# A mixture-of-experts kernel whose last stretch is ranked by explicit waits: left sums, right products between stored groups, last rows in stores of 3, 6 and 9

## The chip, the cores and the metric

The kernel runs on one core of one Trainium2 chip. The metric is the device time of one execution, in microseconds (us). The kernel before takes 205.71 us, the median of three runs (205.70 to 205.94).

A core has five instruction streams that run side by side and meet through semaphores: TensorE (PE, matrix products; its weight loads are shown as PEld), VectorE (DVE), ScalarE (ACT), GpSimd (POOL) and SyncE (SP), which here issues all the transfers. Transfers run on 16 DMA engines. Products land in the eight banks of PSUM; VectorE and ScalarE copy them to SBUF, and from SBUF they are stored to HBM.

## The reference

An attention with pooled keys and values feeds a soft mixture of experts:

```python
logits = x @ phi                                  # x: 4608 x 512, phi: 512 x 32
d = softmax(logits, axis=0)                       # over the 4608 rows
slot_input = d.T @ x                              # 32 slots, 4 for each of 8 experts
for e in range(8):
    h = np.maximum(slot_input[e] @ w1[e], 0.0)    # 4 x 1024, w1[e]: 512 x 1024
    slot_out[e] = h @ w2[e]                       # w2[e]: 1024 x 512
c = softmax(logits, axis=1)                       # over the 32 slots
return c @ slot_out                               # 4608 x 512, float32
```

Everything is float32. The weights w1 and w2 are 33.6 MB, the output is 9.4 MB. The change touches only the end: the second products of the experts, the transposes of `c`, and the last product with its stores.

## The kernel before

The program isn't written in the order in which it runs. Every piece of work is handed to a planner (`Plan.add`) with its engine, an assumed cost, what it reads and writes, and a rank. `Plan.order` then goes through an assumed time line and takes, each time, the piece that can start first; of those that can start at once, the one with the lowest rank. The order that comes out is the order of the instructions on each engine. An engine executes its instructions in that order and waits where an operand is not there yet.

The attention runs over four pairs of batches and is the first two thirds of the time. It leaves the logits, one tile for each pair (`L[0]` to `L[3]`), and the slot inputs `SIM`. What follows is the part that matters here.

- **First products.** `expert_in` multiplies the slots with `w1`, two loads of 1 MB for each expert; `hidden` applies the maximum and turns the result into `hTb`.
- **Second products.** `w2` comes as 16 pieces of 1 MB, two for each expert. A piece serves the left half of the 512 output columns (d = 0, sum in the bank `kvbank`) and the right half (d = 1, sum in `scbank`). `mult` (line 1396) makes eight matrix instructions for one piece and one half. The first 12 pieces are loaded whole (8 KB in a row for each partition). The last four (`NT = 4`, the tails) are loaded in halves by `tail_out`: for each half of the columns and each tail two loads of 256 KB with 1 KB in a row, all the left ones ahead of all the right ones.
- **Keep-warm products.** `keep_warm` (line 1382) adds a product whose result nobody reads, with the lowest rank, for the pieces 6 to 11 and for seven of the eight tail products: 13 in all.
- **Slot weights.** `slots(bp)` computes the softmax over the 32 slots for a pair (VectorE, ScalarE), splits it into a rounded part and a rest, and transposes both on TensorE (line 1508, five matrix instructions for a pair) into `cT[bp]`. Two buffers hold the splits, so that of pair 3 waits for the transposes of pair 1. For the first pair it also keeps an exact transposed copy `c4` of the first three rows j (`ND = 3`). The transposes of pairs 1 to 3 have a rank (`TURN = 30000`) behind that of all other work of the end.
- **Slot sums.** `slot_sums` copies a bank to SBUF (line 1311), adds its four row groups with one product (line 1320), and ScalarE and VectorE split the sum into a rounded part and a rest, `sr` (lines 1577 and 1582).
- **Output.** A partition holds nine output rows, j = 0 to 8, for each pair of batches, 36 in all. `direct` (line 1555) makes the left half of rows 0 to 2 of pair 0 from `c4` and the bank's copy, without waiting for the slot sums, and stores each by itself (line 1567, 128 KB). The other rows come from `out_mult` (line 1591): two matrix instructions for each row. `evict` copies a product to SBUF, rows with odd j on ScalarE (line 1546) and rows with even j on VectorE (line 1547). Three rows form a group. The first six groups (`NA = 6`) are made and stored in halves, left halves first (384 KB a store with 1 KB in a row, line 1603); the other six groups are made at full width and stored as 768 KB with 6 KB in a row.

All loads and stores go through SP's one queue. Which right products stand between which output rows is left to the planner's time line; all have lower ranks than the output rows and are taken as soon as it thinks that their load has landed.

The lines of the code that the change and the prediction touch: `NT, NA` 1290, `slot_sums` 1306, `keep_warm` 1379, `mult` 1389, `expert_out` 1405, `tail_out` 1424, `slots` 1452, `direct` 1550, `out_mult` 1588, `store` 1600, the loops over groups 1610 to 1641.

Of the kernel before, what the change touches and what calls it, by code (L numbers as in the profile page):

```python
# [20 lines left out]
class Plan:  # L21
# [23 lines left out]

    def add(self, eng, cost, fn, r=(), w=(), also=(), pri=None, dma=0.0, slack=0.0):
        cost, ni = cost if isinstance(cost, tuple) else (cost, 4)
# [29 lines left out]
        self.ops.append((eng, cost, fn, deps, pri, dma, tiles, need, slack, ni))  # L77

    def order(self):
# [189 lines left out]
def kernel(  # L269
# [24 lines left out]
    nc = tc.nc  # L294
# [950 lines left out]
    def over(shape, n):  # L1245
# [43 lines left out]
    EG = 4  # L1289
    NT, NA = 4, 6  # L1290
    hTb = hTs.tile().split(E // EG)
# [13 lines left out]

    def slot_sums():
        for d in range(2):
            x = slice(d * HD, d * HD + HD)
            add(
                *((ACT, act(HD)) if d else (DVE, dve(HD))),  # L1310
                lambda d=d, x=x: (nc.scalar.copy if d else nc.vector.tensor_copy)(
                    accs.ap[:, x], pacc[d].ap[:, 0, :HD]
                ),
                r=[pacc[d]], w=[accs.part(d)],
            )
            if d == 0:
                direct(0, 1)
            add(
                PE, 0.5,
                lambda d=d, x=x: nc.tensor.matmul(  # L1320
                    so[d].ap[:, :HD], rep.rearrange("p a n -> p (a n)"), accs.ap[:, x],
                    start=True, stop=True,
                ),
                r=[accs.part(d), rep_b], w=[so[d]],
            )

# [97 lines left out]
    def tail_out():  # L1424
        for d in range(2):
            for e, i, t in tails:
                w2h = w2[e].rearrange("(i p j t) d -> p i j t d", i=2, j=2, t=2)
                for j in range(2):
                    load(
                        lambda j=j, d=d, t=t: t.ap.rearrange("p (j t d) -> p j t d", j=2, t=2)[  # L1430
                            :, j, :, d * HD: d * HD + HD
                        ],
                        w2h[:, i, j, :, d * HD: d * HD + HD], 1 << 18, t.part(2 * d + j),
                    )
        for d in range(2):
            for e, i, t in tails:
                add(
                    PE, (0.45, 16),
                    lambda d=d, e=e, i=i, t=t: mult(pacc[d].ap[:, 0], e, i, t, d),
                    r=[hTb.part(e // EG), t.part(2 * d), t.part(2 * d + 1)], w=[pacc[d]],  # L1440
                )
                if (d, e, i) != (1, E - 1, 1):
                    keep_warm([t.part(2 * d), t.part(2 * d + 1)])

# [3 lines left out]
    cT = {}  # L1448
    TURN = 30000
    c4 = c4s.tile()  # L1450

    def slots(bp):
# [82 lines left out]
    for e in range(E):  # L1535
        expert_out(e)
        if e < NBP:
            slots(e)
    tail_out()


# [7 lines left out]

    def direct(i0, i1):  # L1550
        for i in range(i0, i1):
            po, ot = b_o.tile(), half[0]
            add(
                PE, 0.45,
                lambda po=po, i=i: nc.tensor.matmul(
                    po.ap[:, :HD], c4.ap[:, i * P: i * P + P], accs.ap[:, :HD],
                    start=True, stop=True,
                ),
                r=[accs.part(0), c4], w=[po], also=[ot],
            )  # L1560
            add(
                *evict(lambda i=i: ot.ap[:, i * DM: i * DM + HD], po, HD, i % 2),
                r=[po], w=[ot.part(i)],
            )
            add(
                SP, 0.06,
                lambda i=i: nc.sync.dma_start(outv[:P, i, :HD], ot.ap[:, i * DM: i * DM + HD]),
                r=[ot.part(i)], dma=P * HD * 4 / HALF_RATE,
            )

    outv = out.rearrange("(p j) d -> p j d", j=J)
    slot_sums()
    direct(1, ND)
    for d in range(2):
        x = slice(d * HD, d * HD + HD)
        add(
            ACT, act(HD), lambda x=x, d=d: nc.scalar.copy(sr.ap[:, 0, x], so[d].ap[:, :HD]),
            r=[so[d]], w=[sr.part(d)],
        )
        add(  # L1580
            DVE, dve(HD),
            lambda x=x, d=d: nc.vector.tensor_tensor(
                sr.ap[:, 1, x], so[d].ap[:, :HD], sr.ap[:, 0, x].bitcast(F32), op=ALU.subtract
            ),
            r=[so[d], sr.part(d)], w=[sr.part(d)],
        )

    def out_mult(bp, j, po, x):
# [10 lines left out]

    def store(bp, j0, x, ot, r):  # L1600
        add(
            SP, 0.06,
            lambda: nc.sync.dma_start(
                outv[bp * P: bp * P + P, j0: j0 + G, x],
                ot.ap.rearrange("p (g d) -> p g d", g=G)[:, :, x],
            ),
            r=r, dma=P * G * (x.stop - x.start) * 4 / (DMA_RATE if x.stop - x.start == DM else HALF_RATE),
        )

    for d in range(2):  # L1610
        x = slice(d * HD, d * HD + HD)
        for (bp, j0), ot in zip(groups, half):
            if (bp, j0, d) == (0, 0, 0):
                continue
            for i in range(G):
                po = b_o.tile()
                add(
                    PE, 0.22,
                    lambda po=po, bp=bp, j=j0 + i, x=x: out_mult(bp, j, po, x),
                    r=[sr.part(d), cT[bp]], w=[po], also=[ot],  # L1620
                )
                y = i * DM + d * HD
                add(
                    *evict(lambda ot=ot, y=y: ot.ap[:, y: y + HD], po, HD, (j0 + i) % 2),
                    r=[po], w=[ot.part(G * d + i)],
                )
            store(bp, j0, x, ot, [ot.part(G * d + i) for i in range(G)])
    for bp, j0 in groups[NA:]:
        ot = ots.tile().split(G)
        for i in range(G):  # L1630
            po = b_o.tile()
# [8 lines left out]
            )  # L1640
        store(bp, j0, slice(0, DM), ot, [ot])

# [30 lines left out]
```

## Time and profile before

| what | value |
|---|---|
| median of three runs | 205.71 us |
| the profiled execution's own time | 205.98 us |
| its span, first to last instruction | 204.1 us |
| its instructions | 6131 |
| TensorE busy | 176.8 us (87% of the span) |
| VectorE busy | 134.6 us (66%) |
| ScalarE busy | 70.3 us (34%) |
| DMA, mean over the span | 375 GB/s |
| read from HBM / written | 66.65 MB / 9.44 MB |

The profile is one execution. Times in it are counted from the start of its span. The view by stretches gives, for each stretch of time, the busy time of each engine with the number of its instructions, the granted clock of TensorE (1.00 is full speed), the mean busy share of the 16 DMA engines, and what they moved in GB/s. The chain of waits is followed back from the last instruction: at each step to whatever released it. A line number stands for the line of the program that made the instruction.

### The profile page before, as it was taken

How to read it: one execution, taken by the hardware profiler on the slowest of the kernel's cores; microseconds unless marked ns; L12 is line 12 of the kernel's file. 1: busy time of each engine (PE TensorE's matmuls, PEld its weight loads, DVE VectorE, ACT ScalarE, POOL GpSimd, SP SyncE). 2: the span in 40 equal slices, each digit the busy share in tenths (PEclk: the TensorE clock that was granted, in tenths of full speed). 3: DMA queues.
4: the chain of work that ended last, by engine and by line, in shares of the span. 5: the costliest groups of instructions: out<-in, count | busy, mean ns of one | idle time of the engine just before them, and what ended most of it. 6: DMA issues, size and time to landing. Idle time of an engine off the chain costs nothing.

```text
span 204.1 us, 6131 instructions
## 1 busy us (share of the span) xinstructions
PE 176.8 (87%) x2645; PEld 114.5 (56%) x2645; DVE 134.6 (66%) x243; ACT 70.3 (34%) x188; POOL 84.3 (41%) x84
## 2 busy tenths in 40 slices
PE   7999638988699899798999788989999999999960
PEld 6677535646456486455575456455566635576640
DVE  7822540799897899999899985579942004578600
ACT  2022404446441855517373250201202005466400
POOL 7199205589992994799844482000000000000000
PEclk9999996999969999999999999999999999999995
DMA  6999999999999999999999999999999999599993
GB/s 203 368 391 392 382 387 384 386 387 382 395 382 390 384 391 388 384 396 398 406 392 413 409 409 409 414 430 413 425 413 422 372 311 333 198 338 340 412 410 151
DMA packets 33579, 76.49 MB, mean 375 GB/s; under 512 B 2064, under 2 KB 14864, under 8 KB 32016
## 3 DMA queue, kind: packets, MB, share of 16 engines
q1 hardware_dynamic: 33552, 76.09, 99.1%
q8 instruction: 21, 0.34, 0.7%
q14 instruction: 6, 0.05, 0.1%
HBM read 66.65 MB, written 9.44 MB: 373 GB/s over the span
## 4 chain that ended last, share of the span: by engine, by line
PE 38%; DMA 22%; DVE 14%; POOL 11%; issue 4%; SPq 4%; ACT 2%; POOLq 1%; DVEq 0%
DMA arena<-in_moe_w_dram 14%; DMA arena<-in_v_dram 9%; PE bank L1591 6%; PE scbank L811 6%; PE kvbank L702 4%; PE bank L880 4%; SPq L500 4%; POOL arena L846 3%; POOL arena L667 3%; PE scbank L1382 3%; POOL arena L646 3%; POOL arena L869 3%; PE bank L1008 2%; DVE arena L604 2%; DVE arena L825 2%
## 5 line engine op out<-in xcount | busy, mean ns | idle before, releaser
L646 POOL TENSOR_TENSOR arena<-arena 128x1152 f32<-128x1152 f32 x8 | 21.0, 2636 | 17.7 <-ACT arena L639 15.2
L589 DVE STREAM_TRANSPOSE arena<-top 128x1152 f32<-128x1152 f32 x16 | 21.6, 1354 | 8.2 <-DMA top<-in_q_dram 8.2
L702 PE MATMUL kvbank<-arena 64*32 64x128 f32 x1152 | 21.0, 278 | 6.5 <-issue 2.3
L811 PE MATMUL scbank<-arena 64*64 64x288 f32 x256 | 23.7, 447 | 2.3 <-DVE arena L825 2.3
L518 PE MATMUL kvbank<-ones 128*128 128x256 f32 x82 | 23.6, 424 | 2.4 <-ACT arena L726 1.3
L667 POOL TENSOR_TENSOR arena<-arena 128x128 f32<-128x128 f32 (+2 forms) x32 | 23.4, 732 | 3.2 <-ACT arena L655 1.3
L702 PEld LDWEIGHTS kvbank<-arena 64*32 64x32 f32 x1152 | 16.5, 107 | 11.1 <-issue 5.3
L869 POOL TENSOR_TENSOR arena<-arena,ssm 128x576 f32<-128x576 f32 x16 | 18.3, 1153 | 9.5 <-DVE ssm L865 7.9
L846 POOL TENSOR_TENSOR arena<-arena,smx 128x576 f32<-128x576 f32 x16 | 18.4, 1155 | 7.7 <-DVE smx L841 7.7
L604 DVE TENSOR_REDUCE arena<-arena 128x128 f32<-128x1152 f32 x8 | 17.1, 2151 | 4.4 <-DMA arena<-in_phi_dram 4.2
L880 PE MATMUL bank<-arena 128*128 128x288 f32 x64 | 18.8, 425 | 1.2 <-DVE arena L872 0.8
L518 PEld LDWEIGHTS kvbank<-ones 128*128 128x128 f32 x82 | 15.8, 208 | 6.1 <-ACT arena L726 1.7
L1547 DVE COPY arena<-bank 128x256 f32<-128x256 f32 (+1 forms) x30 | 14.2, 509 | 5.5 <-PE bank L1591 3.7
L825 DVE STREAM_TRANSPOSE arena<-scbank 128x576 f32<-128x576 f32 x16 | 12.2, 764 | 5.6 <-PE scbank L811 5.6
L811 PEld LDWEIGHTS scbank<-arena 64*64 64x64 f32 x256 | 9.9, 141 | 10.2 <-DVE arena L825 3.7
L1591 PE MATMUL bank<-sr,cT 64*128 64x256 f32 (+1 forms) x102 | 14.6, 355 | 0.5 <-DVE arena L1547 0.3
L851 ACT ACTIVATE arena<-arena 128x576 f32<-128x576 f32 x16 | 10.9, 684 | 11.2 <-POOL arena L846 11.1
L880 PEld LDWEIGHTS bank<-arena 128*128 128x128 f32 x64 | 11.2, 189 | 6.4 <-DVE arena L872 1.8
L1336 PE MATMUL bank<-arena,SIM 128*32 128x256 f32 x224 | 13.2, 390 | 0.4 <-DVE SIM L1231 0.4
L1591 PEld LDWEIGHTS bank<-sr,cT 64*128 64x128 f32 x102 | 10.1, 185 | 5.6 <-DVE arena L1547 4.4
L872 DVE STREAM_TRANSPOSE arena<-arena 128x576 f32<-128x576 f32 x16 | 11.9, 752 | 1.3 <-POOL arena L869 1.3
L856 DVE TENSOR_REDUCE ssm<-arena 128x18 f32<-128x576 f32 x16 | 11.8, 739 | 1.1 <-ACT arena L851 0.8
(139 smaller groups left out, 255.9 us busy)
## 6 DMA issues: line engine op xcount, KB each, us to landing
arena<-in_moe_w_dram SPq DMA_DIRECT2D x26, 1024.0 KB, 14.8
top<-in_q_dram SPq DMA_DIRECT2D x8, 1152.0 KB, 12.3
arena<-in_k_dram SPq DMA_DIRECT2D x8, 1152.0 KB, 10.1
arena<-in_v_dram SPq DMA_DIRECT2D x8, 1152.0 KB, 12.6
arena<-in_phi_dram SPq DMA_DIRECT2D x8, 576.0 KB, 7.1
out_dram<-arena SPq DMA_DIRECT2D x6, 768.0 KB, 8.9
out_dram<-arena SPq DMA_DIRECT2D x11, 384.0 KB, 3.2
arena<-in_moe_w_dram SPq DMA_DIRECT2D x16, 256.0 KB, 5.7
```

Of the source, the lines that this page charges most:

```text
L518: lambda: nc.tensor.matmul(warm.ap, ones, ones.unsqueeze(1).to_broadcast([P, 2, P]), start=True, stop=True,),
L589: lambda: nc.vector.transpose(qT.ap.rearrange("p (i u y) -> p u i y", i=2, y=Y), qt.ap[:, h * QT_SZ: h * QT_SZ + QT_SZ].rearrange("p (u i ...
L604: lambda: nc.vector.tensor_reduce(mx.ap[:, c0:c1], ph().rearrange("p c j m -> p c m j"), axis=AX.X, op=ALU.max),
L646: lambda: nc.gpsimd.tensor_tensor(ph(), ph(), mb.ap[:, c0:c1].unsqueeze(2).to_broadcast([P, c1 - c0, J, M]), op=ALU.subtract,),
L667: plus = lambda o, x, y: nc.gpsimd.tensor_tensor(o, x, y, op=ALU.add)
L702: nc.tensor.matmul(acc.ap[M * c: M * c + M, a, : 2 * D], ph()[h0: h0 + HALF, c, j, :], kv()[h0: h0 + HALF, :, c, j * D: j * D + D], start= ...
L811: nc.tensor.matmul(scb.ap[HALF * g: HALF * g + HALF, a, :JY], pair[g].kd.ap[h0: h0 + HALF, i, c].rearrange("p r m -> p (r m)"), pair[g].qT ...
L825: lambda: nc.vector.transpose(ex.ap[:, c * PART: (c + 1) * PART].rearrange("p (a x) -> p a x", a=2), scb.ap[:, :, :JY],),
L846: lambda: nc.gpsimd.tensor_tensor(exv(), exv(), bc(mx), op=ALU.subtract),
L869: lambda: nc.gpsimd.tensor_tensor(exv(), exv(), bc(sm), op=ALU.mult),
L880: nc.tensor.matmul(lp.ap[:, :JY], vpb.ap[:, h, :], aT.ap[:, a * JY: (a + 1) * JY], start=(h == 0), stop=(h == H - 1),)
L1591: nc.tensor.matmul(po.ap[:, : x.stop - x.start], cT[bp].ap[y: y + HALF, j // 2 * P: j // 2 * P + P], sr.ap[y: y + HALF, t, x], start=(t == 0),
```

## The change

- `Plan.add` takes a list `after` of further pieces of work to wait for, and returns the number of the piece.
- Five tails instead of four: piece 11 too is loaded in halves.
- The transposes of pairs 1 and 2 come after the left product of the first tail, those of pair 3 after that of the second (`TURN`); their rank is now an ordinary one.
- `slot_sums(d)` does one half whole, splitting included. The left half comes first, ahead of `direct`.
- `direct` makes two rows instead of three. The third row of the first group is made by `out_mult`, and stored by itself.
- The right product of the first tail comes after the second `direct` row; those of the second and third after the left half of group 1; those of the fourth and fifth after that of group 2 (`RIGHT`). Then the right half's slot sums.
- The tail products have no keep-warm products any more; six are left, for the pieces 5 to 10.
- The 18 rows of pairs 2 and 3 are stored by 3, 6 and 9 rows (6, 12 and 18 KB in a row for each partition) instead of six times 3. The two large ones get areas of their own in SBUF.

```diff
-    def add(self, eng, cost, fn, r=(), w=(), also=(), pri=None, dma=0.0, slack=0.0):
+    def add(self, eng, cost, fn, r=(), w=(), also=(), pri=None, dma=0.0, slack=0.0, after=()):
...
+        deps.update(after)
...
+    b0 = W0 + NOUT * OT_SZ
+    big = {6: area(b0, [6 * DM], 1, [ws]), 9: area(b0 + 6 * DM, [9 * DM], 1, [ws])}
...
-    ND = 3
+    ND = 2
...
-    NT, NA = 4, 6
+    NT, NA = 5, 6
+    TURN = {1: 0, 2: 0, 3: 1}
+    RIGHT = (-1, 1, 1, 2, 2)
+    SLOT_AT = (20.06, 20.08, 20.1)
...
+    def slot_sums(d, middle=lambda: None):
+        x = slice(d * HD, d * HD + HD)
...
+        add(
+            ACT, act(HD), lambda: nc.scalar.copy(sr.ap[:, 0, x], so[d].ap[:, :HD]),
+            r=[so[d]], w=[sr.part(d)],
+        )
...
-                if (d, e, i) != (1, E - 1, 1):
-                    keep_warm([t.part(2 * d), t.part(2 * d + 1)])
+
+    def tail_mult(d, n, after=()):
+        e, i, t = tails[n]
+        return add(
+            PE, (0.45, 16), lambda: mult(pacc[d].ap[:, 0], e, i, t, d),
+            r=[hTb.part(e // EG), t.part(2 * d), t.part(2 * d + 1)], w=[pacc[d]], after=after,
+        )
...
-                pri=TURN + 10 * bp + t if bp >= 1 else None,
+                after=turn_at[bp],
...
-        if e < NBP:
-            slots(e)
+        if e == 0:
+            slots(0)
     tail_out()
+    for n in range(NT):
+        x = tail_mult(0, n)
+        for bp in range(1, NBP):
+            if TURN[bp] == n:
+                turn_at[bp].append(x)
+    for bp in range(1, NBP):
+        plan.at(SLOT_AT[bp - 1])
+        slots(bp)
+    plan.at(21)
...
+    z = slot_sums(0)
+    for i in range(ND):
+        z = direct(i, [z])
+    for n in range(-1, NA):
+        if n >= 0:
+            z = half_group(0, n, n == 0)
+        for m in range(NT):
+            if RIGHT[m] == n:
+                tail_mult(1, m, [z])
+        if RIGHT[NT - 1] == n:
+            slot_sums(1)
+    for n in range(NA):
+        half_group(1, n)
+    for bp, j0, n in ((2, 0, 3), (2, 3, 6), (3, 0, 9)):
+        ot = (ots if n == G else big[n]).tile().split(n)
+        for i in range(n):
...
-        store(bp, j0, slice(0, DM), ot, [ot])
+        store(bp, j0, slice(0, DM), ot, [ot], None, n)
```

`half_group(d, n, single)` makes the rows of one group's half as the loop before did; with `single` it starts at row `ND` and stores each row by itself.

More of the change, by code (lines that the diff above doesn't have):

```diff
@@ L1304 @@
     so = [b_l.tile(), Tile(ap=kvbank[:, 1])]
[L1306 to L1325, printed above, removed]
+    def slot_sums(d, middle=lambda: None):
+        x = slice(d * HD, d * HD + HD)
+        add(
+            *((ACT, act(HD)) if d else (DVE, dve(HD))),
+            lambda: (nc.scalar.copy if d else nc.vector.tensor_copy)(
+                accs.ap[:, x], pacc[d].ap[:, 0, :HD]
+            ),
+            r=[pacc[d]], w=[accs.part(d)],
+        )
+        y = middle()
+        z = add(
+            PE, 0.5,
+            lambda: nc.tensor.matmul(
+                so[d].ap[:, :HD], rep.rearrange("p a n -> p (a n)"), accs.ap[:, x],
+                start=True, stop=True,
+            ),
+            r=[accs.part(d), rep_b], w=[so[d]], after=[y] if y is not None else (),
+        )
+        add(
+            ACT, act(HD), lambda: nc.scalar.copy(sr.ap[:, 0, x], so[d].ap[:, :HD]),
+            r=[so[d]], w=[sr.part(d)],
+        )
+        add(
+            DVE, dve(HD),
+            lambda: nc.vector.tensor_tensor(
+                sr.ap[:, 1, x], so[d].ap[:, :HD], sr.ap[:, 0, x].bitcast(F32), op=ALU.subtract
+            ),
+            r=[so[d], sr.part(d)], w=[sr.part(d)],
+        )
+        return z
     def expert_in(e, hb):
@@ L1434, in tail_out @@
                     )
[L1435 to L1441, printed above, removed]
-                if (d, e, i) != (1, E - 1, 1):
-                    keep_warm([t.part(2 * d), t.part(2 * d + 1)])
+    def tail_mult(d, n, after=()):
[3 more added lines that the diff above has]
+            r=[hTb.part(e // EG), t.part(2 * d), t.part(2 * d + 1)], w=[pacc[d]], after=after,
+        )
     cmxs = sb("cmx", [P, J], 1)
@@ L1448 @@
     cT = {}
-    TURN = 30000
+    turn_at = {bp: [] for bp in range(NBP)}
     c4 = c4s.tile()
@@ L1548, in evict, with direct @@
         )
[L1550 to L1578, printed above, removed]
-        )
-        add(
[L1581 to L1585, printed above, removed]
-        )
+    def direct(i, after=()):
+        po, ot = b_o.tile(), half[0]
+        x = add(
+            PE, 0.45,
+            lambda: nc.tensor.matmul(
+                po.ap[:, :HD], c4.ap[:, i * P: i * P + P], accs.ap[:, :HD],
+                start=True, stop=True,
+            ),
+            r=[accs.part(0), c4], w=[po], also=[ot], after=after,
+        )
+        add(
+            *evict(lambda: ot.ap[:, i * DM: i * DM + HD], po, HD, i % 2 == 0),
+            r=[po], w=[ot.part(i)],
+        )
+        store(0, i, slice(0, HD), ot, [ot.part(i)], i)
+        return x
     def out_mult(bp, j, po, x):
@@ L1598, in out_mult, with store @@
             )
-    def store(bp, j0, x, ot, r):
+    def store(bp, j0, x, ot, r, i=None, g=G):
+        n, k = (g, 0) if i is None else (1, i)
         add(
@@ L1608, in store @@
         )
[L1610 to L1626, printed above, removed]
-            store(bp, j0, x, ot, [ot.part(G * d + i) for i in range(G)])
@@ L1628, with half_group @@
-    for bp, j0 in groups[NA:]:
-        ot = ots.tile().split(G)
-        for i in range(G):
+    def half_group(d, n, single=False):
+        (bp, j0), ot, x = groups[n], half[n], slice(d * HD, d * HD + HD)
+        for i in range(ND if single else 0, G):
+            po = b_o.tile()
+            z = add(
+                PE, 0.22, lambda po=po, j=j0 + i: out_mult(bp, j, po, x),
+                r=[sr.part(d), cT[bp]], w=[po], also=[ot],
+            )
+            y = i * DM + d * HD
+            add(
+                *evict(lambda y=y: ot.ap[:, y: y + HD], po, HD, (j0 + i) % 2),
+                r=[po], w=[ot.part(G * d + i)],
+            )
+            if single:
+                store(bp, j0 + i, x, ot, [ot.part(G * d + i)], i)
+        if not single:
+            store(bp, j0, x, ot, [ot.part(G * d + i) for i in range(G)])
+        return z
@@ new lines @@
+    outv = out.rearrange("(p j) d -> p j d", j=J)
+    z = slot_sums(0)
[14 more added lines that the diff above has]
+        for i in range(n):
```

7 lines of the change are left out of this document (4 added, 3 removed).

## The prediction

> **What bounds the kernel now.** I read the page first, then its last third by stretches, the chain of waits there, and SP's transfers.
>
> ```profile
> span 204.1 us, 6131 instructions
> PE 176.8 (87%) x2645; PEld 114.5 (56%) x2645; DVE 134.6 (66%) x243; ACT 70.3 (34%) x188; POOL 84.3 (41%) x84
> q8 instruction: 21, 0.34, 0.7%
> ```
> ```profile
> 150.00:157.00 7.00, 7.00 (x127) 4.70 (x123) 1.58 (x4) 1.63 (x5) 0.00 (x0) 1.00 1.02 425
> 167.00:172.00 5.00, 4.99 (x47) 2.43 (x41) 1.72 (x4) 2.40 (x9) 0.00 (x0) 1.00 1.06 346
> 172.00:173.00 1.00, 1.00 (x8) 0.68 (x4) 0.04 (x1) 0.19 (x1) 0.00 (x0) 1.00 0.93 313
> 173.00:175.00 2.00, 2.00 (x18) 0.99 (x17) 0.94 (x3) 0.69 (x3) 0.00 (x0) 1.00 0.55 184
> 175.00:177.00 2.00, 2.00 (x25) 1.07 (x24) 1.23 (x4) 0.89 (x3) 0.00 (x0) 1.00 0.36 117
> 177.00:189.00 12.00, 11.48 (x85) 8.21 (x82) 9.41 (x22) 7.57 (x19) 0.00 (x0) 1.00 1.02 340
> 190.00:200.00 10.00, 6.99 (x32) 5.27 (x30) 1.98 (x3) 1.33 (x3) 0.00 (x0) 0.99 1.02 412
> 200.00:201.00 1.00, 0.00 (x0) 0.00 (x0) 0.00 (x0) 0.00 (x0) 0.00 (x0) 0.50 0.80 326
> 201.00:202.00 1.00, 0.00 (x0) 0.00 (x0) 0.00 (x0) 0.00 (x0) 0.00 (x0) 0.50 0.06 25
> ```
>
> The last two columns tell the story. Whole pieces come at 425 GB/s, halves with 1 KB in a row at 346, and stores leave at 340 (1 KB) and 412 (6 KB). The transfers are the bound everywhere but from 173 to 177, where they move 368 + 234 = 602 KB in 4 us: at 340 GB/s that is 1.8 us of work, so 2.2 us are lost. There the loads are through and the stores not yet made. From 176.7 an unbroken stream of stores sets the end: eleven half groups of 393 KB (1.157 us each at 340) and 18 full rows of 262 KB (11.45 us at 412) end at 176.7 + 12.7 + 11.45 = 200.9, where the rate drops. (Begin of the stream: from 175 to 177 go 234 KB, of which 131 KB are the last single store; the other 103 KB are 0.3 us at 340.)
>
> What delays the stores is TensorE, which has no pause in the chain of waits:
>
> ```profile
> 169.70 0.57 PE kvbank L1396 x8
> 170.27 0.01 issue
> 170.28 0.74 PE bank L1508 x5
> 171.02 0.56 PE bank L1555 x2
> 171.58 0.57 PE scbank L1396 x8
> 172.15 0.63 PE bank L1320 x2
> 172.77 0.43 PE bank L1555 x2
> ...
> 174.40 0.67 PE bank L1591 x6
> 175.07 0.57 PE scbank L1396 x8
> 175.64 0.90 PE bank L1591 x8
> 176.53 0.57 PE scbank L1396 x8
> 177.10 0.68 PE bank L1591 x8
> 177.78 0.63 PE kvbank L1320 x2
> ...
> 179.72 0.45 PE bank L1591 x3
> ...
> 191.61 5.38 PE scbank L1382 x24
> ```
>
> The last left product ends at 170.27. Three rows cost 0.67, four 0.90, a right product 0.57, a slot sum 0.63.
>
> SP's issues give the pace of the loads and the way from a product to its store (line 500 from 164 on, then the stores of groups 1 and 3):
>
> ```profile
> L500 SPq DMA_DIRECT2D arena<-in_moe_w_dram x9: 368/368/697, 164.0 to 169.5; - x9
> DMA to landing us min/median/max: 5.5/5.7/5.7
> ```
> ```profile
> L1603 SPq DMA_DIRECT2D out_dram<-arena x1: 659/659/659, 175.5 to 175.5; - x1
> L1603 SPq DMA_DIRECT2D out_dram<-arena x1: 372/372/372, 178.1 to 178.1; - x1
> ```
>
> Half loads are issued every (169.5 - 164.0)/8 = 0.69 us and land 5.7 later, so eight are in flight and a ninth waits for the first. Group 1's last product ends at 175.07 and its store is issued at 175.5; group 3's at about 177.45 (half of the four rows behind the right product after 176.53) and 178.1. I take 0.6. From issue to moving bytes: 176.7 - 175.5 = 1.2 with an issue of 0.66; with the usual 0.37, 0.9.
>
> **The change part by part.**
>
> *The fifth tail.* One whole piece (1.05 MB, 2.47 us at 425) leaves the queue ahead of the left halves, four half loads come in, two of them left ones. The left half is complete 2.47 - 2 x 0.69 = 1.1 us sooner, at T = 169.2. The last right half lands 4 x 0.69 - 2.47 = 0.3 later, at 175.5. The price of the slower bytes is between this 0.3 and 1.05/0.346 - 2.47 = 0.56; the loads' end on the DMA engines moves from about 173.0 to 173.4.
>
> The Trainium skill (DMA: Bandwidth & Descriptors, "Why small descriptors are slow (HBM only)") gives a fixed cost of about three 32-byte beats for each packet: estimated from it, 1 KB would run at 35/32 and 8 KB at 259/256 of the ideal time, an 8% difference. The rows show 425 against 346, 23%. By the rule the piece would cost 0.2 us, and the change would look 0.2 to 0.3 better; the measured rows decide.
>
> *The transposes of pairs 1 to 3*, five instructions each, 2.27 us together, move ahead of T:
>
> ```profile
> 163.90:171.10 7.20, 2.27 (x15) 1.53 (x15) 1.00 0.99 322
> ```
> ```profile
>   DMA arena<-in_moe_w_dram: 2.6, 6
> ```
>
> TensorE's tail products waited 2.6 us in all for loads between 163.9 and 170.2 (second fence, what line 1396 was idle for). A right product of piece 11 (0.6) leaves that stretch too. So they fit; if this cover is gone, they cost up to the 0.74 that now stands behind the last left product.
>
> *From T to the stream.* The bank's copy on VectorE, with 0.07 and 0.06 around it, is now waited for, since nothing else is ranked there:
>
> ```profile
> 170.34 0.42 DVE L1311 COPY cS<-kvbank 128x256 f32<-128x256 f32 x1 [0.20 <-PE kvbank L1396]
> ```
>
> TensorE then goes: 169.75, slot sum to 170.38, two direct rows (0.56 and 0.43) to 171.37, right product to 171.94, the single row and group 1 (four rows) to 172.84, two right products to 173.98, group 2 to 174.65, the fourth right product to 175.22; the fifth waits for its load at 175.5, to 176.07; group 3 to 176.74. The second slot sum (0.63) either comes ahead of group 3's third row or behind it; I take half, 177.05. Behind that fifth product stand all rows on TensorE, and for those waits SP with every store. Store of group 3: 177.65, moving at 178.55. Single stores and groups 1 and 2 (1.15 + 2.31 of work from 173.4) are through by 177.3, so about 1.3 us are still lost ahead of group 3, besides 0.3 ahead of group 2. From there on each group takes TensorE 0.67 and the transfers 1.157, and the stream is unbroken: nine half groups 10.4, then the 18 rows.
>
> *The wait for eight transfers back* binds nothing: group 3's is the sixth store, eight back is the 18th half load, landed at 175.5 - 2 x 0.69.
>
> *Stores of 3, 6 and 9 rows.* Their data: the 18 right half rows and 18 full rows took TensorE from 179.72 to 191.61. Sooner by the 0.4 of group 3 and with 0.6 to the issue, the nine rows are issued near 191.8 and moving at 192.7, while the six before them keep the engines busy until 200.3 - 5.7 = 194.6: hidden by 1.9 us. No row shows 12 or 18 KB packets. Bounds: the 8 KB rate of 425 instead of 412 on 15 rows gives -0.3; the only packets of 16 KB are the instruction queue's (0.34 MB/21), which take 0.7% of 16 x 204.1/21 = 1.09 us each, 15 GB/s for an engine against 412/16 = 26, which would give +7. Those go elsewhere; the nearest row is the 8 KB load. I take -0.1.
>
> *Keep-warm products.* Twelve of 13 run after the last row (x24 from 191.61 to 197.0, under the stores), so seven fewer are worth nothing at the end. They hold no clock either: it is 1.00 through the stretch without them, and 0.50 where TensorE idles. Were it to fall to that, rows would take 0.45 us and cost the whole gain. The smaller `c4`, the ranks of `slots` and the buffers cost nothing: VectorE works 1.72 of 5 us from 167 to 172 and 9.41 of 12 from 177 to 189.
>
> *Sum.* Before, group 3 stood at 176.7 + 2 x 1.157 = 179.0 in the stream; after, 178.55: -0.5. With -0.1 for packets, -0.6. Against the profiled execution's 205.98 (span 204.1 and 1.9 around it) 205.4; the median of the runs lies 0.3 lower, so 205.1. Bounds: slot sum behind the row and no wait for the fifth load, -0.6 (204.5); slot sum wholly ahead and some of the transposes late, +0.5 (205.6).
>
> **The rivals.**
>
> *The lag of one engine goes (203.3).* After 200.9 the rate is 25 GB/s, one engine of 16 (412/16 = 26): one runs 1.8 us behind, and the end waits for it.
>
> ```profile
> q1 hardware_dynamic: 91, 0.47, 95.4%
> q8 instruction: 1, 0.02, 4.9%
> ```
> ```profile
> L1382 PE MATMUL scbank<-ones x26: 379/379/484, 179.0 to 196.6; 128*128 128x256 f32 x26
> ```
>
> These are the queues from 195 to 196.2: an instruction packet there takes an engine for about a microsecond. The page has 21 such packets for 5290 products and weight loads, one for 252, and this last one comes within the last two dozen. The change drops 44: seven keep-warm products of four (26/13 products, as many weight loads), and 16 for the shorter `c4`. It might never be fetched, or after the stores. Against it: it is fetched ahead of its use, by how much no row says, and may come all the same, with the same lag. 205.1 - 1.8 = 203.3.
>
> The Trainium skill (the same page, "Queues, rings and completion order") says that an engine takes its queues in turn, packet by packet, which agrees with one engine held up while the others go on.
>
> *The right products hold the rows (206.3, slower).* The break-even is a store of group 3 at 200.9 - 11.35 - 10.4 - 0.9 = 178.25. If the transposes land behind the left products as five do now (0.74), and the second slot sum stands wholly ahead of group 3 (0.3), its store comes at 178.7 and the gain turns to +0.4; with the fifth load late by as much, since its queue is now shared with seven stores, +0.9. For it: five right products are explicitly ahead of group 3, and only four were in all. Against: 2.6 us of waiting are there to take the transposes.
>
> *The order comes out as it was (205.7).* The chain shows right products between rows already. If the left half comes 1.1 sooner but the extra right product (0.57) and the slower bytes (0.56) eat it, nothing is left.
>
> *Large packets are slow (over 206).* As bounded above; it would decide from 1.5% of the last 9.5 us on, and little speaks for it.
>
> **How the numbers follow.** Forecast 0.42, lag gone 0.25, slower by the right products 0.15, unchanged 0.13, large packets 0.05. A measurement of this kernel can tell 0.2%, 0.41 us, from no change: faster is below 205.30. The forecast's own range (204.5 to 205.6) puts two thirds of it there, so faster 0.28 + 0.25 = 0.53; same 0.12 + 0.11 and a part of the small losses, 0.25; slower 0.22. The range goes from the lag's 203.3 less 0.2 to the slower rival's 206.3.
>
> **What would show it.** Right: the left bank's copy near 169.2; the first store before 171.6; group 3's store between 177.2 and 178; a second dip of the rate between 176 and 178.5; one engine's 25 GB/s for under 2 us at the end. Wrong: no dip at all; the last instruction packet gone and with it the tail of 25 GB/s; transposes (line 1508 before) behind the last left product; a rate away from 412 in the last 10 us; a pause between the six rows' and the nine rows' packets.

## The result: 202.46 us

The changed kernel takes 202.46 us (median of six runs, 202.39 to 202.58), against 205.93 us for the kernel before beside it (205.70 to 206.06). The ratio is 0.9834, with a 95% interval of 0.9821 to 0.9847: 3.5 us faster. The forecast was 205.1, in a range from 203.1 to 206.3, so the time lies below the whole range. The profiled execution after took 202.39 us.

The page of the changed kernel:

```profile
span 200.6 us, 6083 instructions
PE 172.5 (86%) x2623; PEld 111.0 (55%) x2623; DVE 134.4 (67%) x243; ACT 70.3 (35%) x188; POOL 84.3 (42%) x84
q8 instruction: 20, 0.33, 0.7%
```

There are 44 TensorE instructions fewer (2 x 2645 before, 2 x 2623 now), as the diff promises, and 20 instruction packets instead of 21. The view by stretches; the columns are those of the prediction, and the last two are what to read (busy share of the DMA engines, and GB/s):

```profile
171.00:173.00 2.00, 2.00 (x33) 1.12 (x32) 1.24 (x4) 0.68 (x3) 0.00 (x0) 1.00 1.09 357
173.00:175.00 2.00, 2.00 (x27) 1.17 (x20) 0.76 (x2) 0.37 (x1) 0.00 (x0) 1.00 1.08 373
175.00:177.00 2.00, 2.00 (x24) 1.24 (x20) 1.24 (x4) 1.27 (x4) 0.00 (x0) 1.00 0.92 314
180.00:181.00 1.00, 0.82 (x9) 0.59 (x8) 0.74 (x3) 0.65 (x2) 0.00 (x0) 1.00 0.50 174
190.00:197.00 7.00, 2.24 (x9) 1.35 (x8) 1.27 (x2) 0.59 (x1) 0.00 (x0) 0.97 1.00 424
198.00:199.00 1.00, 0.00 (x0) 0.00 (x0) 0.00 (x0) 0.00 (x0) 0.00 (x0) 0.50 0.69 295
199.00:200.00 1.00, 0.00 (x0) 0.00 (x0) 0.00 (x0) 0.00 (x0) 0.00 (x0) 0.50 0.01 0
```

Three things differ from before. From 173 to 177 the transfers move 373 and 314 GB/s where they moved 184 and 117, and a short dip is left at 180. The last stretch runs at 424 instead of 412. And the rate falls from 295 to nothing; the stretch at 25 GB/s that ended the kernel before isn't there. The chain of waits shows TensorE's order (start, length, line, instructions; line 1413 from 171 on are right products, 1399 an unread product, 1325 the slot sums, 1578 the direct rows, 1594 the other rows):

```profile
168.32 0.63 PE kvbank L1413 x6
168.95 0.63 PE scbank L1399 x2
169.58 0.61 PE bank L1325 x2
170.19 0.86 PE bank L1578 x4
171.05 0.57 PE scbank L1413 x8
171.62 0.68 PE bank L1594 x8
172.30 1.00 PE scbank L1413 x16
173.30 0.67 PE bank L1594 x6
173.96 0.75 PE scbank L1413 x8
174.72 0.66 PE bank L1594 x6
175.38 0.63 PE scbank L1413 x8
176.01 0.68 PE bank L1594 x8
176.69 0.63 PE kvbank L1325 x2
```

Group 1 stands complete at 172.30, where it was 175.07 before, and group 3 (the six instructions from 174.72) is made ahead of the fifth right product, not behind it. Its store:

```profile
L1607 SPq DMA_DIRECT2D out_dram<-arena x1: 372/372/372, 176.0 to 176.0; - x1
```

### The profile page after: what moved, and what is told of

It reads as the page before. It is cut to its first block, busy times and chain, and to the rows that moved or that the text cites. A ratio compares the mean times of both kernels' runs of the same rounds, so it can differ in the third digit from the quotient of the medians.

```text
span 200.6 us, 6083 instructions
## 1 busy us (share of the span) xinstructions
PE 172.5 (86%) x2623; PEld 111.0 (55%) x2623; DVE 134.4 (67%) x243; ACT 70.3 (35%) x188; POOL 84.3 (42%) x84
## 4 chain that ended last, share of the span: by engine, by line
PE 34%; DMA 26%; DVE 13%; POOL 11%; issue 4%; SPq 4%; ACT 2%; POOLq 1%; DVEq 0%
DMA arena<-in_moe_w_dram 18%; DMA arena<-in_v_dram 8%; PE bank L1594 6%; PE scbank L813 6%; PE kvbank L704 5%; SPq L502 4%; PE bank L882 4%; POOL arena L848 3%; POOL arena L669 3%; POOL arena L648 3%; POOL arena L871 3%; PE bank L1010 2%; DVE arena L606 2%; DVE arena L827 2%; DVE arena L874 2%
## 5 line engine op out<-in xcount | busy, mean ns | idle before, releaser
L1570 ACT COPY arena<-bank 128x256 f32<-128x256 f32 (+1 forms) x24 | 10.3, 445 | 8.4 <-PE bank L1594 7.0
```

## The experiments

All times are medians, and each ratio is to runs of the kernel before on the same chip. Where a ratio is turned into microseconds, it is times 205.9.

### The lag of one engine

Unread products (as the keep-warm ones) are added at the end of the changed kernel, behind the last row, 12 or 6 of them, and taken from the kernel before:

```diff
+    for _ in range(12):            # e1_pad12; 6 in e1_pad6
+        add(PE, WC, <the unread product>, r=[ones_b, ot], w=[cool], pri=FILL + 30)
```
```diff
-            if 2 * e + i >= 2 * E - NT - 6:        # e2_before_lean, on the kernel before
-                keep_warm([t])
...
-                if (d, e, i) != (1, E - 1, 1):
-                    keep_warm([t.part(2 * d), t.part(2 * d + 1)])
```

> The changed kernel with twelve more unread products (48 TensorE instructions) behind its last output row, so that TensorE's stream has 2 instructions more than in the kernel before. Lag theory (1.8 us of the gain come from the last instruction packet, which is no longer fetched while the stores leave): the page shows 21 instruction packets again instead of 20, one DMA engine ends alone at 25 GB/s for 1.5 to 2 us, time 204.0 to 204.4. Rival (the lag went because of the large stores, or by chance): 202.3 to 202.7.

> The changed kernel with six more unread products (24 instructions) behind its last output row: the same kind of work as with twelve, but TensorE's stream stays short of the kernel before by 22 instructions. Lag theory: 20 packets if the packet is asked for where that count is reached, and 202.3 to 202.7; 21 packets and 204.0 to 204.4 if it is asked for more than five instructions ahead. Rival (more products cost time by themselves): half of what twelve cost.

> The kernel before without its 13 keep-warm products (52 TensorE instructions fewer), nothing else changed. Lag theory: 20 instruction packets, no engine left alone at the end, 203.8 to 204.3. Rival (they held the clock, or the lag is the small stores'): 205.7 to 206.1 or more, with 25 GB/s at the end.

Measured: with 12 more 204.36 us (0.9916, 0.9900 to 0.9933), with 6 more 202.57 (0.9827, 0.9811 to 0.9844), the kernel before without its 13 204.32 (0.9916, 0.9893 to 0.9938). Two rows of each page, in this order:

```profile
PE 178.2 (88%) x2647; PEld 116.1 (57%) x2647; DVE 134.4 (66%) x243; ACT 70.3 (35%) x188; POOL 84.2 (42%) x84
q8 instruction: 21, 0.34, 0.7%
```
```profile
PE 174.0 (87%) x2635; PEld 112.9 (56%) x2635; DVE 134.3 (67%) x243; ACT 70.4 (35%) x188; POOL 84.3 (42%) x84
q8 instruction: 20, 0.33, 0.7%
```
```profile
PE 172.5 (85%) x2619; PEld 111.4 (55%) x2619; DVE 134.5 (66%) x243; ACT 70.5 (35%) x188; POOL 84.3 (42%) x84
q8 instruction: 20, 0.33, 0.7%
```

The kernel with 12 more, by stretches:

```profile
199.00:200.00 1.00, 0.00 (x0) 0.00 (x0) 0.00 (x0) 0.00 (x0) 0.00 (x0) 1.00 0.09 37
200.00:201.00 1.00, 0.00 (x0) 0.00 (x0) 0.00 (x0) 0.00 (x0) 0.00 (x0) 1.00 0.04 18
```

Between 5270 and 5290 products and weight loads a 21st packet comes, and with it the stretch at one engine's pace. It costs 204.36 - 202.57 = 1.8 us; taken from the kernel before, it gives (1 - 0.9916) x 205.9 = 1.7. The 24 products and weight loads that six unread products bring, without the packet, cost nothing that can be measured. About half of the change's 3.5 us is this: a program that became a little shorter. The records of the single packets in the traces show the lag itself. In the kernel before, all but the last few packets are through by 201.0 us, and those come one behind the other, 6 KB each, until 202.7; with 12 more the others are through by 199.4, and the last come singly, 18 KB each, until 201.1; with 6 more all end by 199.3. That the engine that is behind is the one that fetched is inferred, since the records name no engine. The packet itself took 0.94 and 0.96 us; why the lag is 1.7 to 1.8 no run shows.

### The large stores

```diff
-    for bp, j0, n in ((2, 0, 3), (2, 3, 6), (3, 0, 9)):      # e4_stores_by_3, on the changed kernel
+    for bp, j0, n in ((2, 0, 3), (2, 3, 3), (2, 6, 3), (3, 0, 3), (3, 3, 3), (3, 6, 3)):
```
```diff
-    for bp, j0 in groups[NA:]:             # e12_before_lean_369, on the kernel before without its 13
+    for bp, j0, n in ((2, 0, 3), (2, 3, 6), (3, 0, 9)):
```

> The changed kernel with the last 18 rows stored six times by 3 (768 KB, 6 KB in a row) as before. Lag theory: 20 instruction packets, no engine left alone, and only the larger packets' own gain is lost: 0.1 to 0.3 us, 202.5 to 202.8. Rival (the lag went because three large stores replaced six): 204.0 to 204.4, with 25 GB/s at the end.

> The kernel before without its thirteen unread products (which by itself took away the lag of one engine and ran 204.32 us) and with its last rows stored by 3, 6 and 9 instead of six times 3; the computation is complete. Theory that the parts add: 204.32 less the 0.4 to 0.5 us that the large stores were worth on the changed kernel, 203.7 to 204.0 us, which leaves 1.2 to 1.5 us of the change to the order of the rows and right products. Rival, that the large stores are worth something only where the queue never ran dry: 204.2 to 204.5 us.

Measured: 202.99 us (0.9845, 0.9830 to 0.9860) and 203.94 (0.9905, 0.9884 to 0.9925). The stretch of the full rows, in the changed kernel with stores of three, and in the kernel before without its 13 and with the large stores:

```profile
190.00:197.00 7.00, 2.49 (x11) 1.36 (x8) 1.50 (x3) 0.73 (x2) 0.00 (x0) 1.00 1.02 416
```
```profile
190.00:197.00 7.00, 1.61 (x8) 0.76 (x6) 1.98 (x3) 1.30 (x3) 0.00 (x0) 0.86 1.02 427
```

The medians put the large stores at 0.5 us on the one and 0.4 on the other kernel, the ratios at 0.2 on both, and the intervals of both pairs overlap. This stretch is too short to give the rate of 18 KB packets: with stores of 3, 6 and 9 it reads from 418 GB/s (12 unread products more) to 435 (e9). The whole stream of the 18 full rows (262 KB each) is the better measure. From its first packet to its last it takes 11.38 us in the changed kernel and 11.67 with stores of three; in the kernel before without its 13, 11.42 with the large stores and 11.63 (e2) without. So the large stores are worth 0.2 to 0.3 us: 413 to 415 GB/s against 404 to 406. The Trainium skill ("DMA: Bandwidth & Descriptors", "Why small descriptors are slow (HBM only)") gives a fixed cost of some three beats of 32 bytes a packet; estimated from it, 18 KB packets would gain 1% on 6 KB ones, 0.1 us here. The streams show about 2%.

### What stands ahead of group 3

The left rows of groups 3 to 5 are held behind the fifth right product alone (e9), or behind it and the right slot sum (e3):

```diff
     for n in range(-1, NA):
         if n >= 0:
-            z = half_group(0, n, n == 0)
+            z = half_group(0, n, n == 0, held)     # every row's product with after=held
...
+                held = [last]                      # e9_held_one: the fifth right product
+                held = [last, slot_sums(1)]        # e3_held: and the right slot sum
```

> The changed kernel with the order that the prediction assumed: the left halves of groups 3 to 5 are held behind the fifth right product and the right half's slot sum. If the prediction's sum failed because group 3 stood ahead of that product: store of group 3 near 177.7 instead of 176.0, about 1 us more of idle transfers between 175.5 and 178.5, 203.1 to 203.7. Rival (the order behind group 2 doesn't matter, the transfers have enough queued): 202.3 to 202.7.

> The changed kernel with the left halves of groups 3 to 5 held behind the fifth right product alone (not behind the slot sum, as in the run before). That is the order of the prediction's sum: store of group 3 near 177.0, about 0.8 us more of idle transfers: 203.1 to 203.5. If the time of the run before came from the wait for the bank's copy and the slot sum, this one keeps less than half of its loss of 2.8 us. Rival: as that run, 205 or more.

Measured: behind the fifth product alone 203.23 us (0.9869, 0.9846 to 0.9893), behind both 205.35 (0.9964, 0.9951 to 0.9977). The chain and the store of group 3 with the fifth product alone:

```profile
174.17 0.57 PE scbank L1413 x8
174.74 0.63 PE scbank L1399 x2
175.37 0.70 PE scbank L1413 x8
176.06 0.67 PE bank L1594 x7
176.74 0.63 PE kvbank L1325 x2
```
```profile
L1607 SPq DMA_DIRECT2D out_dram<-arena x1: 372/372/372, 177.4 to 177.4; - x1
```

This is the order that the prediction worked out, and the fifth product and group 3 end when it said, at 176.06 and 176.74, with the store 0.6 later. Ahead of that the rows run up to 0.5 us sooner than in the working (the fourth product ends at 174.74, forecast 175.22); both meet again at the fifth load, and here an unread product fills the wait for it. The order costs 0.0035 x 205.9 = 0.7 us against the changed kernel, half of the 1.4 that the store is later; the likely reason is that the changed kernel has its own dip at 180, which this one hasn't. Part of the 0.7 may not be the order's: from 160 to 173, ahead of any difference in it, the transfers of this execution ran at 315 GB/s and those of the changed kernel at 331.

Held behind both, the loss was 2.9 us where 0.6 to 1.2 were expected:

```profile
175.49 0.67 PE scbank L1413 x8
176.16 0.64 PE scbank L1399 x2
...
176.83 0.38 ACT cS L1317
177.21 0.04 issue
177.25 0.70 PE kvbank L1325 x2
```

Behind the fifth product came an unread product, the right bank's copy on ScalarE and only then the sum: 2.5 us, from 175.49 to 177.95, in which TensorE made no row. The expectation had left the copy and the unread product out.

### Which part gives the order its gain

Between the kernel before without lag and with large stores (203.94) and the changed kernel lie 1.5 us. First, single parts undone on the changed kernel:

```diff
-    NT, NA = 5, 6                                  # e5_four_tails
+    NT, NA = 4, 6                                  # with RIGHT = (-1, 1, 1, 2)
```
```diff
-                after=turn_at[bp],                 # e6_late_turn
+                pri=30000 + 10 * bp + t if bp >= 1 else None,
```
```diff
-                tail_mult(1, m, [z])               # e7_free_right
+                tail_mult(1, m)
```
```diff
-    ND = 2                                         # e11_three_direct
+    ND = 3                                         # group 0 then has no row of its own
```

> The changed kernel with four tails instead of five (the right products stand behind the second direct row, group 1, group 1 and group 2). If the early left half carries the gain: left bank's copy about 1 us later (near 170.1 instead of 169.0), first store after 172, transfers idle about 1 us more between 173 and 178, less 0.4 for the faster bytes: 202.9 to 203.5. Rival (the fifth piece in slow packets is a loss, the order alone is enough): 201.9 to 202.3.

> The changed kernel with the transposes of pairs 1 to 3 ranked behind all other work again. If TensorE's work behind the left half sets the stores: the transposes of pair 3 (five instructions, 0.74 us) fall behind the left half's copy and the first stores come 0.3 to 0.8 later: 202.8 to 203.4. Rival (they only fill TensorE's pauses): 202.3 to 202.7.

> The changed kernel with its five right products no longer bound behind anything (they may start as soon as their half piece is there); the computation is complete. The planner then puts the first of them ahead of the left slot sum and one between each two groups. Theory that rows ahead of right products is what fills the transfers: each right product that comes sooner pushes the rows behind it by 0.5 to 1.2 us, but the group that was late in the kernel before, group 3, already stands where it stood; 202.6 to 203.4 us. Rival, that the explicit bounds are worth nothing because the ranks alone give the order: 202.3 to 202.6 us, as the changed kernel. Rival, that the bounds are worth most of the gain beside the lag of one engine: 203.7 us or more.

> The changed kernel with three rows of the first group multiplied straight from the copied sums, as before the change, instead of two; the computation is complete. Theory: the third such product took 0.63 us on TensorE and delays group 1 and all that stands behind it by about 0.4 us, so 202.7 to 203.0 us if the transfers run dry there. Rival: the third store is issued sooner than the single row of the changed kernel and nothing is lost: 202.3 to 202.6 us.

Measured: four half pieces 202.67 us (0.9852, 0.9819 to 0.9885); transposes by rank 202.37 (0.9818, 0.9804 to 0.9833); right products free 202.90 (0.9852, 0.9834 to 0.9871); three direct rows 202.90 (0.9859, 0.9834 to 0.9884). Every interval touches that of the changed kernel. None of them carries 1.5 us; the transposes' bounds carry nothing. The time with four half pieces lies between its two expectations and bears out neither.

Then parts undone together: the bounds of the transposes and of the right products (e16); these and the fifth piece (e13); with the slots' tables at their old rank and three direct rows too (e18); and with all right products and the second slot sum ranked ahead of the rows as before (e17), which leaves of the change only the left slot sum ahead of the direct rows, and the large stores (and small things: six unread products, and which engine copies a direct row):

```diff
+    for m in range(NT):                            # e17_sum_first_only, beside the edits of e18
+        tail_mult(1, m)
     z = slot_sums(0)
     for i in range(ND):
         z = direct(i, [z])
+    slot_sums(1)
...
-        for m in range(NT):
-            if RIGHT[m] == n:
-                tail_mult(1, m, [z])
-        if RIGHT[NT - 1] == n:
-            slot_sums(1)
```

> The changed kernel with its five half pieces, but with the transposes by rank alone and the right products bound behind nothing; the computation is complete. If explicit bounds on both are what keeps TensorE on the rows, 203.3 us or more; if the ranks alone do, as the run with only the right products free showed, 202.5 to 203.0 us.

> The changed kernel with three parts undone at once: four pieces in halves instead of five, the transposes by rank alone instead of behind left products, the right products bound behind nothing. What is left of the change are the slot sums by halves, two direct rows instead of three, and the stores by 3, 6 and 9; the computation is complete. If the three parts cover for one another, most of the 1.5 us comes back: 203.5 to 204.0 us. If the gain of the order lies in the split slot sums, with the left half's rows ranked ahead, it stays: 202.5 to 203.1 us, the first store before 172.3 and no long stretch at 100 to 200 GB/s between 173 and 177.

> The kernel with three parts undone, and also with the slots' tables back at their old rank and three direct rows; what is left of the change are the left slot sum ahead of the direct rows, the right products ranked behind the rows, and the stores by 3, 6 and 9. The computation is complete. If the third direct row (0.56 us on TensorE ahead of group 1, less the row of 0.17 that it stands for) is what sets the start of the stream: 203.2 to 203.5 us. If it is not, 202.8 to 203.1 us as without it.

> As the kernel with the slots' tables back and three direct rows, and also with the right products and the second slot sum ranked ahead of the rows as before the change; what is left of the change are the left slot sum ahead of the first direct row and the stores by 3, 6 and 9. The computation is complete. If the rank of the right products carries the rest, 203.7 to 204.0 us as the kernel before with large stores and no lag; if the place of the slot sum does, 203.0 to 203.5 us.

Measured, with the steps between them:

| kernel | us | ratio, 95% interval | step |
|---|---|---|---|
| before, no lag, large stores (e12) | 203.94 | 0.9905 (0.9884 to 0.9925) | |
| + left slot sum ahead of the direct rows (e17) | 204.14 | 0.9905 (0.9888 to 0.9923) | 0.0 us |
| + right products and right sum ranked behind rows (e18) | 203.26 | 0.9867 (0.9851 to 0.9883) | 0.8 |
| + two direct rows, slots' tables later (e13) | 202.95 | 0.9847 (0.9829 to 0.9865) | 0.4 |
| + fifth half piece (e16) | 203.13 | 0.9852 (0.9837 to 0.9867) | -0.1 |
| + both bounds, that is the changed kernel | 202.46 | 0.9834 (0.9821 to 0.9847) | 0.4 |

The two stretches that were empty before, in e17, e18 and e13:

```profile
173.00:175.00 2.00, 2.00 (x24) 0.98 (x16) 0.56 (x2) 1.02 (x3) 0.00 (x0) 1.00 0.55 176
175.00:177.00 2.00, 2.00 (x28) 1.42 (x24) 1.09 (x3) 0.72 (x2) 0.00 (x0) 1.00 0.34 110
```
```profile
173.00:175.00 2.00, 2.00 (x32) 0.99 (x24) 0.42 (x1) 0.86 (x3) 0.00 (x0) 1.00 0.76 253
175.00:177.00 2.00, 2.00 (x28) 1.42 (x24) 1.09 (x3) 0.78 (x3) 0.00 (x0) 1.00 0.63 213
```
```profile
173.00:175.00 2.00, 2.00 (x28) 1.45 (x24) 1.00 (x3) 0.84 (x3) 0.00 (x0) 1.00 0.64 221
175.00:177.00 2.00, 2.00 (x20) 1.00 (x18) 1.57 (x5) 1.19 (x4) 0.00 (x0) 1.00 0.95 307
```

The first is the gap of the kernel before, 184 and 117 GB/s, to within 6%. In e17 two right products stand on TensorE ahead of group 1, among the direct rows; ranked behind the rows (e18) only one does, group 1's store is issued at 174.5 instead of 175.0, and the gap is half filled. With one direct row fewer (e13) the stretch from 175 to 177 nearly closes; that from 173 to 175 doesn't. The rank of the right products is the only single step whose two intervals don't touch. The traces agree on the whole: the first full row begins to move at 189.4 us in e12 and e17, 188.8 in e18, 188.1 in e13, 188.5 in e16 and 187.9 in the changed kernel, 1.5 us from end to end. The other steps are at the edge of what these runs tell apart (e16 fell between its two expectations, e17 a little above both), and the split of the last 0.3 to 0.4 us among the fifth piece and the two bounds stays open.

### The dip that is left at 180

The first right row needs VectorE's subtraction for the second slot sum, and that stands behind a copy of the last row of group 5 on VectorE:

```profile
177.83 0.42 DVE L1571 COPY arena<-bank 128x256 f32<-128x256 f32 x1 [0.55 <-PE bank L1594]
178.17 0.41 DVE L1337 TENSOR_TENSOR sr<-kvbank,sr 128x256 fp32r<-128x256 f32 x1
```

Two suspects: that copy, and the two unread products on TensorE at the same time:

```profile
177.76 1.06 PE scbank L1399 x4
```

The subtraction ends at 178.58 and these at 178.82, when the first right row starts: they end within 0.3 us of each other, so one alone may gain nothing. The unread products are taken away (e10), the copy is given to ScalarE (e14), or both (e15):

```diff
-            if 2 * e + i >= 2 * E - NT - 6:        # e10_no_warm, e15_sum_first_lean
-                keep_warm([t])
```
```diff
-                *evict(..., po, HD, (j0 + i) % 2), # e14_sum_first, e15_sum_first_lean
+                *evict(..., po, HD, (j0 + i) % 2 or (d, n, i) == (0, NA - 1, G - 1)),
```

> The changed kernel without its six unread products behind the loads; the computation is complete, and TensorE's stream falls from 5284 to 5260 instructions, so the number of instruction packets stays at 20. Theory: the unread product at 177.76 to 178.82 us stands on TensorE ahead of the last products, and the short dip of the transfers at 180.5 to 181 us (47 GB/s for half a microsecond) shortens by some 0.2: 202.1 to 202.4 us. Rival: without them the granted clock falls in the stage of the rows and the left half ends later: 202.8 us or more. No difference (202.4 to 202.6 us) says that they cost and bring nothing.

> The changed kernel with one eviction moved: the last row of group 5 is copied by ScalarE instead of VectorE, so that VectorE's subtraction for the right half (178.17 to 178.58 us, behind that copy) can start 0.4 us sooner; one of the two unread products behind the slot sum moves to the end too. The computation is complete. If the dip at 180.5 us comes from the subtraction, the first store of the right half is issued 0.3 to 0.5 us sooner and the time is 202.0 to 202.3 us. If the unread product still stands ahead, or the products behind that row wait for their banks anyway, 202.4 to 202.6 us.

> As the kernel with that one eviction moved, and without the six unread products; the computation is complete. The run without them alone showed a granted clock of 0.50 from 183 to 187 us and rows that took 0.8 us longer in all, and no other time. If the sooner subtraction shortens TensorE's pauses enough to hold the clock, 201.9 to 202.3 us; if the clock falls again, 202.4 to 202.8 us.

Measured: without the products 202.55 us (0.9834, 0.9802 to 0.9865), the copy moved 202.17 (0.9804, 0.9789 to 0.9818), both 202.01 (0.9799, 0.9782 to 0.9815). The subtraction, and the second of the dip, with the copy moved:

```profile
177.58 0.42 DVE L1337 TENSOR_TENSOR sr<-kvbank,sr 128x256 fp32r<-128x256 f32 x1 [0.48 <-ACT sr L1332]
```
```profile
180.00:181.00 1.00, 0.83 (x8) 0.77 (x8) 0.74 (x3) 0.43 (x2) 0.00 (x0) 1.00 1.01 335
```

The subtraction starts 0.6 us sooner and the dip is gone, 335 GB/s for 174. The planner also moved one of the two unread products away in e14, so e14 alone doesn't part the two suspects. Without any unread product they part: with the copy in its place (e10) the first right row still waits for the subtraction, until 178.86, and the dip stays, 231 GB/s from 180 to 181; with the copy moved (e15) it is gone, 347. So the copy is what has to move (by these traces; the intervals of the two times overlap). The kernels with the copy moved are about 0.6 us faster than the changed one (0.9804 against 0.9834; the two intervals don't touch) and beat both kernels of this document; between the two of them there is no difference that can be told.

With the unread products alone taken away (e10), the granted clock (first of the last three columns) was 0.50 from 181.4 to 188.2 us. One row from that stretch, one from behind it, and the same stretch of the changed kernel:

```profile
183.00:185.00 2.00, 2.00 (x13) 1.90 (x13) 1.27 (x3) 0.74 (x2) 0.00 (x0) 0.50 1.01 338
189.00:192.00 3.00, 3.00 (x17) 1.75 (x16) 2.78 (x5) 2.02 (x4) 0.00 (x0) 1.00 0.89 365
```
```profile
189.00:192.00 3.00, 3.00 (x16) 1.85 (x12) 2.04 (x4) 1.45 (x3) 0.00 (x0) 1.00 1.04 432
```

While the clock is low the transfers keep 338 GB/s: enough rows are there. But the rows fall behind, the store of six rows is issued at 189.6 us instead of 187.9, and then the transfers run dry: the 18 full rows take 11.96 us instead of 11.38, and this execution 202.88. The median, 202.55, shows no loss, but its four runs lie far apart and go with their mean granted clock: 203.17 and 202.88 us at 0.940 and 0.951, 202.22 and 201.90 at 0.962 and 0.963. Only the second was traced, so what the clock costs in the others isn't shown. With the copy moved as well (e15) the clock is 1.00 in these stretches.

## Why the prediction was wrong

**What bounds the kernel.** Right. The transfers bind everywhere but from 173 to 177, TensorE's order is what delays them there, and 2.2 us were to be had. The order (1.5) and the moved copy of e14 (0.6) together recover most of it.

**Left half complete at 169.2, first store before 171.6.** Right: the last left product ends at 168.95, the direct rows follow at 170.19, and the first store is issued at 171.1. But the fifth half piece was worth nothing that can be told: with four the time is 202.67, and the two intervals overlap.

**"Behind that fifth product stand all rows on TensorE".** This step failed. The new argument bounds a right product from below, behind a group; nothing bounds a row behind a right product. The planner was free to put group 3 ahead of the fifth product, and did (probably because its time line had that load late; the time line isn't on record). The forecast put group 3's store at 177.65 and it came at 176.0; of these 1.65 us most is the fifth product, the wait for its load and the half slot sum, which the working had ahead of it. The two dips (0.3 and 1.3 us) that were to remain became smaller ones, at 176 and at 180. With the order as forecast (e9) the chain meets the working again at the fifth load. Its 203.23 with 1.8 for the lag is 205.0, where the forecast was 205.1. That is closer than the parts warrant, and partly luck: e9's interval is half a microsecond to each side, and the large packets were put too low. But it fits with the order and the tail as the two main misses.

**The lag of one engine stays.** This failed, and is the larger miss: 1.7 to 1.8 us. The rival had the mechanism, the count of instructions and the price (1.8) right, with a chance of 0.25. What spoke for it was in the trace before, and the working names it: one packet for each so many TensorE instructions, and the last one within two dozen instructions of the end, with 44 dropped. The reason set against it, that the packet may come all the same, had no row behind it. The runs showed 20 packets and no tail.

**Large packets, -0.1.** Right sign, a little small: 0.2 to 0.3 by the streams of full rows, though the times alone don't tell it from nothing. The nine rows' store was issued at 191.5, forecast 191.8, and nothing paused between it and the six rows.

**The transposes, the smaller `c4`.** The transposes cost nothing, as forecast. The sum has no term of its own for the direct row that was dropped, though its order counts only two; the runs put it at 0.4 to 0.5 (the step from e18 to e13, which moves the slots' tables too, and e11), at the edge of what they tell apart. It stood on TensorE ahead of group 1, with 0.43 to 0.56 us as the other direct rows in the chain before, against 0.17 for a row from `out_mult`.

**"They hold no clock either".** Right for the seven that the change drops, and for all 13 of the kernel before: in the changed kernel and in e2 the clock is 1.00 from 173 to 192. Not for the six that stay: without them it fell to 0.50 for 6.8 us. The price for that, the whole gain, was too high: the traced execution lost 0.6 us in its full rows.

**The rivals.** Right products holding the rows, the order as it was, and slow large packets are all out. The order as it was does come back, gap and all, but only once the ranks are taken back too (e17).

**The sum by what was measured,** from the ladder of ratios: lag 1.7, large stores 0.2, rank of the right products 0.8, one direct row fewer 0.4, bounds and fifth piece 0.3. That is 3.4, the whole change by its ratio (3.5 by the medians). The steps are differences along one ladder, so they have to add up to it: the sum is no proof of the single steps.

## What to carry to other kernels

Count instruction packets against instructions before pricing a change that adds or drops some: a packet that falls into the last transfers costs its whole lag, and a handful of instructions decides it. Read a bound in a planner for what it leaves free, not only for what it holds, and work out the order by the planner's own rule. Where a stream of stores runs dry, look on every engine for the one copy that stands ahead of the next dependent step: moving one 0.4 us copy was worth about 0.6 us, more than the large stores. And a clock that falls may be paid for later than where it falls.

## What the runs showed of the hardware

- The end waits for what an instruction packet holds up, though the last row was made long before: 21 packets for 5290 or 5294 products and weight loads, 20 for 5246 or 5270, and 1.7 to 1.8 us between the two.
- A granted clock of 0.50 on TensorE for 6.8 us left the transfers at 338 GB/s while it lasted, and cost 0.6 us behind it, where the rows came late (e10, one traced execution).
- The 18 full rows left at 413 to 415 GB/s in stores with 6, 12 and 18 KB in a row (changed kernel, e12), and at 404 to 406 in stores with 6 KB (e4, e2).
